# Moving the first weight tiles' narrowing, the first key loads and the first one-hots in a clustered attention with two feed-forward blocks

## The chip, the core and the metric

The kernel runs on one core of one Trainium2 chip. The metric is the device time in microseconds (us). A core has TensorE (PE in the rows; its weight loads are PEld), VectorE (DVE), ScalarE (ACT), GpSimd (POOL) and SyncE (SP), which here only issues transfers. Each engine runs its own instructions in their order and waits on semaphores for the others. "q" behind an engine's name in a row (SPq) is its sequencer, which issues transfers.

## What is computed

The reference, cut to what matters (B=2, H=8, S=768, D=64, 16 clusters; the weights arrive as float64):

```python
q_n, k_n, c_n = (x / (norm(x) + 1e-6) for x in (q, k, centroids))
q_assign = argmax(einsum('bhsd,hcd->bhsc', q_n, c_n), -1)   # k_assign likewise
mask = q_assign[:, :, :, None] == k_assign[:, :, None, :]
scores = where(mask, scale * q @ k.T, -1e9)
x = softmax(scores) @ v                                     # to [1536, 512]
x = softplus(x @ w_in) @ w_out                              # d_ff 2048
out = (silu(x @ w_gate) * (x @ w_val)) @ w_out2             # d_ff 1536
```

## The kernel before

A float32 product runs as three products of a split: x = hi + lo, and hi·hi + hi·lo + lo·hi are summed. A split is a copy to hi and a subtraction for lo.

**Attention** goes over 8 pairs of heads (`NP`), 12 tiles of 128 queries to a pair, 96 tiles in all (`N_IT`, index i). `step(i)` writes out, in this order: the scores of tile i on TensorE (`sc`, L466) and their row maximum on VectorE (L474); the exponentials of tile i-1 on ScalarE (`ex`, L482); the six transposes of tile i-2 on TensorE (`tr`, L498), split by ScalarE (`th`, L504) and VectorE (`tl`, L505); the events that a table `at` holds for i (what later pairs need); and a part of the product with the values (`pv`, L515). The program's order on each engine is that in which this code is written.

**The first pair** is prepared ahead of the loop. SyncE issues the loads of the centroids (`cn`, L272), of the first queries `qn` and keys `kn` (`load_qk(0)`, L254) and of the first weight tile `raw` (L94). VectorE and ScalarE normalize the centroids (L301 to L312; two of the steps, L305 and L306, are ScalarE's). TensorE transposes q, then the centroids (`cps`, L318), then k (L340); 12 small products with the centroids (`sims`, L377) follow, q's six and then k's six, into one PSUM tile; between these groups stand 17, 1, 6, 9, 3 and 1 transposes of a constant (`warm`, L280). VectorE splits q and k (L352, L353) and then makes the one-hots of q's and k's clusters in five instructions over both (`prep_arg`, L401 to L423). TensorE transposes the one-hots (`ohps`, L622), VectorE and ScalarE copy them to their places (L627 to L634), and the scores of tile 0 can start.

**Weights** are loaded as bits of float64 and made to float32 in two steps by the generator `w_narrow`: the first step is one ScalarE instruction (L115) and two of VectorE (L116, L119); the second is two of VectorE (L123, L126), the copy to hi (L135, VectorE) and the subtraction for lo (L136, GpSimd). The steps of all tiles stand in a queue `todo`; `pump(n)` writes out the next n. In the attention loop `pump(2)` stands behind tiles 0 and 26 (L708), so that two of the tiles of `w_in` are ready when attention ends; a second step also issues the load of a further tile.

**The feed-forward blocks** (L731, L813, L913) follow and are not touched.

Of the kernel before, what the change touches and what calls it, by code (L numbers as in the profile page):

```python
# [11 lines left out]
F32 = mybir.dt.float32  # L12
# [4 lines left out]
ALU = mybir.AluOpType  # L17
AX = mybir.AxisListType
PSUM = bass.MemoryType.PSUM

# A score of a query and a key of different clusters.  A power of two whose
# unit in the last place is far above any score, so that it swallows the score.
FAR = 2.0 ** 100

# The high words of 2^-126 and of the largest float32 as float64, read as float32.
F64_LEAST = struct.unpack("f", struct.pack("I", 0x38100000))[0]
# [3 lines left out]
def _r(t):  # L30
    """The float32 view of a float32r tile, for engines that read it as data."""
    return t.bitcast(F32)


def _h(ap, n=2):
    """[p, n*m] -> [p, n, m]"""
    return ap.rearrange("p (a n) -> p a n", a=n)
# [3 lines left out]
def kernel(  # L41
# [12 lines left out]
):  # L54
    """Every float32 product runs as float32r products: x = hi + lo exactly, both
    parts being float32r, and hi*hi + hi*lo + lo*hi is accumulated.

    Token order on chip: column b*768 + t*128 + p is token b*768 + 6*p + t.
    """
    nc = tc.nc  # L60
# [26 lines left out]

# [1 line left out]
    def w_load(w, rows, cols):  # L89
# [12 lines left out]
    def w_narrow(loaded):  # L102
        """float64 bits [p, a, f, 2] (low word, high word) -> float32 [p, a, f], in two steps

        For 2^-126 <= |x| < 2^128 the float32 exponent is the top bit and the low
        seven bits of the eleven; magnitudes below and above are brought to that
        range's ends first."""
        raw, shape, wide = loaded
        if not wide:
            yield  # L110
            yield raw
            return
        lo, hi = raw[:, :, :, 0], raw[:, :, :, 1]
        m = wp.tile(shape, I32, tag="m", name="m", bufs=2)
        nc.scalar.activation(out=m.bitcast(F32), in_=hi.bitcast(F32), func=AF.Abs)  # L115
        nc.vector.tensor_scalar(  # L116
            out=m.bitcast(F32), in0=m.bitcast(F32), scalar1=F64_LEAST, scalar2=F64_MOST, op0=ALU.max, op1=ALU.min
        )
        nc.vector.tensor_scalar(  # L119
            out=m, in0=m, scalar1=3, scalar2=0x3FFFFFF8, op0=ALU.logical_shift_left, op1=ALU.bitwise_and  # L120
        )
        yield
        nc.vector.scalar_tensor_tensor(  # L123
            out=m, in0=hi, scalar=-0x40000000, in1=m, op0=ALU.bitwise_and, op1=ALU.bitwise_or
        )
        nc.vector.scalar_tensor_tensor(  # L126
            out=m, in0=lo, scalar=29, in1=m, op0=ALU.logical_shift_right, op1=ALU.bitwise_or
        )
        yield m.bitcast(F32)
# [14 lines left out]

    # units of the two feed-forward blocks; a unit's own tiles are split three units
    # ahead, the tile of the output product with the unit
    NU = NF1 + NF2
# [12 lines left out]

    # the first tiles of the second block's values have room early on
    early = {NF1 - 14 + 3 * i: ("val", i) for i in range(3)}
# [22 lines left out]
    def split_tasks(batch):  # L185
        """two steps for each tile"""
        steps = {}

        def first(key):
            while key not in loaded_t:  # L190
                load_ahead(len(loaded_t) + 1)
            steps[key] = w_narrow(loaded_t.pop(key))
            next(steps[key])

        def second(key, tag):
            x = next(steps[key])
            load_ahead(3)
            pool, bufs = pool_of[tag]
            W[key] = w_split(x, pool, tag, bufs)

        tasks = []
        for key, _, tag in batch:
            tasks.append(functools.partial(first, key))
            tasks.append(functools.partial(second, key, tag))
            begun.add(tasks[-1])
        return tasks

    # work of the other engines that is emitted between parts of the products
    todo = collections.deque()

    def first_do(tasks):
        """before all others, but for the second step of a tile whose first was done"""
        begun_one = [todo.popleft()] if todo and todo[0] in begun else []
        todo.extendleft(reversed(begun_one + tasks))
# [10 lines left out]

    # ================= attention =================
    actx = ExitStack()
# [10 lines left out]

    # operands of the scores, one set per head in flight:
    # Q: [q_lo; -FAR*(1-onehot); 0] and [q_hi; q_hi]  # L240
    # K: [k_hi; onehot; 0] and [k_hi; k_lo]
    NB = 4
# [5 lines left out]
    def load_qk(pr, which=(0, 1)):  # L248
        b, m = divmod(pr, NPAIR)
        for n in which:  # L250
            src, dst, nm = ((q, qn_t, "qn"), (k, kn_t, "kn"))[n]
            t = pre.tile([128, NT, 2, D], F32, tag=nm, name=nm)
            for hh in range(2):
                nc.sync.dma_start(  # L254
                    out=t[:, :, hh, :],
                    in_=src[b, 2 * m + hh].rearrange("(p t) d -> p t d", t=NT),
                )
# [12 lines left out]
    cnc2 = one.tile([128, S], F32, tag="xa0", name="cnc2")  # L270
    cn, c2 = cnc2[:, 0:D], cnc2[:, D:2 * D]
    nc.sync.dma_start(out=cn, in_=centroids.rearrange("h c d -> (h c) d"))  # L272
    load_qk(0)
    load_ahead([1, 1, 3][0])

    def warm(n):
        """the tensor engine's clock rises with its use"""
        ps = ps_o.tile([128, 512], F32, tag="o", name="warm")
# [4 lines left out]

    # constants
    ohs = one.tile([4 * C, 2], F32, name="ohs")
# [12 lines left out]

    # centroids over their norms; the block diagonal of a pair of heads
    ss = one.tile([128, 4], F32, name="ss")  # L300
    nc.vector.tensor_tensor(out=c2, in0=cn, in1=cn, op=ALU.mult)  # L301
    nc.vector.tensor_reduce(out=ss[:, 0:1], in_=c2, axis=AX.X, op=ALU.add)
    nc.vector.tensor_scalar_max(ss[:, 0:1], ss[:, 0:1], 1e-37)
    # a square root to float32's accuracy: an estimate and a Newton step
    nc.scalar.activation(out=ss[:, 1:2], in_=ss[:, 0:1], func=AF.Ln)  # L305
# [16 lines left out]

# [1 line left out]
    xr_t, y_t, eq_t, oh_t, OH_t, VV_t, hl_t = {}, {}, {}, {}, {}, {}, {}  # L324
# [60 lines left out]
    def prep_sims(pr, which, spread=True):  # L385
        """spread: between the transposes of a step"""
        if which == 0:
# [7 lines left out]
    def prep_arg(pr, step):  # L395
        """the one-hot of the first of the largest"""
        full = [128, 4 * NT, C]
# [55 lines left out]

# [1 line left out]
    N_IT = NP * 2 * NT  # L455
    CT = 2                  # query tiles to a chunk of P V
    CW = 128 * CT
# [122 lines left out]

    # the first pair's; its one-hots get 32 partitions to a head, so that they are copied
    # to their places by the engines
    oh0 = two.tile([128, NT, CW], F32R, tag="tl", name="oh0").rearrange("p t n -> p (t n)")[:, 0:128 * NT]
# [16 lines left out]
    khl = two.tile([128, NT, CW], F32R, tag="th", name="khl").rearrange("p t n -> p (t n)")  # L600
    prep_split(0, 1, nc.vector, (khl[:, 0:S], khl[:, S:2 * S]))
    for which in range(2):
# [5 lines left out]
    load_ahead([1, 1, 3][2])  # L608
    # and the start of the second pair's
    mpool[0] = (ps_t, "t")  # L610
# [4 lines left out]
    mpool[0] = (ps_m, "m")  # L615
    for n in range(4):
        prep_arg(0, n)
    for half in range(2):
# [84 lines left out]
    for i in range(N_IT + 1):  # L703
        step(i)
        if i == N_IT - 12:
            rctx.close()
            pool_of["b"] = (ctx.enter_context(tc.tile_pool(name="bp", bufs=4, side="right", reuse_waits="tile")), 4)
        if i in (0, 26):  # L708
            pump(2)
    rec(NP - 1)  # L710
    rec_rows(NP - 1)
    sctx.close()

    # ================= the two feed-forward blocks =================
    psa = tc.tile_pool(name="psa", bufs=4, space=PSUM, side="right", reuse_waits="tile")
# [9 lines left out]
    def proj(xh, xl, w, banks, kks):  # L725
        """banks[c] += (x @ w)^T over the slices kks, for 512 tokens each"""
        hi, lo = w
# [10 lines left out]

    # the first products start with the pairs of heads that are done
    h0 = [bank() for _ in range(NCH)]  # L740
# [31 lines left out]

    # block 1: y^T = softplus(x w_in) w_out
    acc = mp.tile([128, KD, NTOK], F32, tag="acc", name="acc")
# [76 lines left out]

    # block 2: out = (silu(y w_gate) * (y w_val)) w_out2
    acc2 = mp.tile([128, NTOK // 128, DM], F32, tag="acc", name="acc2")
# [88 lines left out]
# Bass has no float64: such an input goes in as its bits, and is narrowed on the chip.  # L942
_INS = ['q', 'k', 'v', 'centroids', 'moe_w_in', 'moe_w_out', 'moe2_w_gate', 'moe2_w_val', 'moe2_w_out']
# [26 lines left out]
```

## Time and profile before

| | us |
|---|---|
| three runs | 860.93, 862.71, 866.04; median 862.71 |
| the profiled execution, from its first to its last instruction (the only time that is on record of it) | 861.7 |
| TensorE busy in it | 820.9 (95%) |
| VectorE, ScalarE, GpSimd busy | 683.9, 397.6, 336.0 |

Times inside the execution count from its first instruction. The attention loop's first scores stand at 18.3 us. A row of a timeline gives start, duration, engine, line, operation, output and inputs, shapes, the count of merged instructions, and in brackets how long the engine had been idle before and what ended that.

### The profile page before, as it was taken

Reading aid. Unit: us, or ns where it says so; the run is one execution under the profiler, and the core shown is the slowest. Engines: PE = TensorE matmul, PEld = TensorE weight load, DVE = VectorE, ACT = ScalarE, POOL = GpSimd, SP = SyncE. Lnnn points to the kernel's source line nnn. Section 1 sums busy time; section 2 is a strip of 40 time slices with the busy share of each in tenths; the row PEclk is TensorE's granted clock in tenths of the full one; section 3 lists DMA queues with packets and bytes.
Section 4 is the critical chain, followed back from the end, with each engine's and each line's share of the span. In section 5 each row is a group of like instructions: output and inputs, shape, how many; then the busy total and the mean of one; then the engine's idle time right before and its main releaser. Section 6 shows DMA issues by size and latency. Waiting matters only on the chain.

```text
span 861.7 us, 11737 instructions
## 1 busy us (share of the span) xinstructions
PE 820.9 (95%) x4366; PEld 697.5 (81%) x4366; DVE 683.9 (79%) x1016; ACT 397.6 (46%) x735; POOL 336.0 (39%) x229
## 2 busy tenths in 40 slices
PE   7999999999999999989898997799999999999998
PEld 6899999999898778768777786588888888888886
DVE  6888978988896778898888888849886868876464
ACT  4689889888893755433244433232212212120210
POOL 3636465555522545444244333424433312332110
PEclk9799999999999999999999999999999999999999
DMA  8975775575312132122221120202312221220003
GB/s 200 248 163 134 190 150 142 141 172 122 85 38 69 49 98 74 51 74 80 65 74 50 49 74 25 68 7 74 97 50 74 74 73 49 74 72 26 1 1 146
DMA packets 65336, 75.42 MB, mean 88 GB/s; under 512 B 28960, under 2 KB 51584, under 8 KB 65280
## 3 DMA queue, kind: packets, MB, share of 16 engines
q1 hardware_dynamic: 65280, 74.68, 32.3%
q8 instruction: 34, 0.56, 0.3%
q14 instruction: 22, 0.18, 0.1%
HBM read 48.27 MB, written 3.19 MB: 60 GB/s over the span
## 4 chain that ended last, share of the span: by engine, by line
PE 60%; DVE 25%; DMA 5%; issue 4%; ACT 4%; POOL 1%; SPq 0%; POOLq 0%; ACTq 0%; DVEq 0%
PE bank L731 28%; PE bank L913 11%; PE sps L466 5%; PE ops L515 5%; DVE m L116 5%; PE tps L498 5%; DVE acc L827 5%; DVE e L796 3%; PE bank L813 2%; DVE r L789 2%; DVE m L126 2%; DVE m L123 2%; DMA rd<-rt 2%; DMA R<-rd 2%; DVE whi L135 2%
## 5 line engine op out<-in xcount | busy, mean ns | idle before, releaser
L136 POOL TENSOR_TENSOR wlo<-m,whi 128x512 fp32r<-128x512 f32 x68 | 100.7, 1480 | 291.9 <-DVE whi L135 266.1
L116 DVE TENSOR_SCALAR m<-m 128x512 f32<-128x512 f32 x68 | 86.0, 1265 | 38.4 <-ACT m L115 38.4
L505 DVE TENSOR_TENSOR tl<-tps,th 128x384 fp32r<-128x384 f32 x192 | 98.8, 550 | 20.2 <-ACT th L504 19.6
L474 DVE TENSOR_REDUCE nm<-sps 128x1 f32<-128x768 f32 x96 | 91.3, 952 | 14.3 <-PE sps L466 11.4
L498 PE MATMUL tps<-id,p 128*128 128x128 f32 x576 | 95.3, 282 | 1.1 <-DVE tl L505 1.1
L504 ACT CAST th<-tps 128x384 fp32r<-128x384 f32 x192 | 84.6, 491 | 20.1 <-PE tps L498 17.1
L482 ACT ACTIVATE p<-sps,nm 128x768 f32<-128x768 f32 x96 | 88.1, 918 | 5.6 <-DVE nm L474 5.6
L466 PE MATMUL sps<-KT,QT 128*128 128x384 f32 x384 | 84.7, 343 | 5.6 <-ACT p L482 3.7
L731 PE MATMUL bank<-YH,whi 128*128 128x512 f32 x288 | 81.6, 391 | 2.5 <-DVE acc L827 2.5
L498 PEld LDWEIGHTS tps<-id,p 128*128 128x128 f32 x576 | 76.4, 153 | 8.4 <-DVE tl L505 5.1
L731 PE MATMUL bank<-YL,whi 128*128 128x512 f32 x288 | 81.6, 392 | 0.0
L731 PE MATMUL bank<-YH,wlo 128*128 128x512 f32 x288 | 81.6, 392 | 0.0
L769 ACT CAST gh<-e 128x1536 fp32r<-128x1536 f32 x16 | 23.7, 1481 | 122.8 <-DVE e L796 122.8
L515 PE MATMUL ops<-th,VV 128*128 128x256 f32 x288 | 79.7, 306 | 0.0
L813 PE MATMUL bank<-gh,whi 128*128 128x512 f32 x192 | 58.9, 407 | 17.3 <-DVE r L789 8.2
L115 ACT ACTIVATE m<-raw 128x512 f32<-128x512 f32 x68 | 44.5, 666 | 62.1 <-POOL wlo L136 62.0
L515 PE MATMUL ops<-tl,VV 128*128 128x256 f32 x288 | 71.9, 279 | 0.0
L770 POOL TENSOR_TENSOR gl<-e,gh 128x1536 fp32r<-128x1536 f32 x16 | 57.1, 3573 | 34.5 <-ACT gh L769 30.7
L466 PEld LDWEIGHTS sps<-KT,QT 128*128 128x128 f32 x384 | 63.4, 191 | 6.7 <-ACT p L482 4.4
L731 PEld LDWEIGHTS bank<-YH,whi 128*128 128x128 f32 x288 | 54.4, 189 | 14.3 <-issue 2.9
L731 PEld LDWEIGHTS bank<-YH,wlo 128*128 128x128 f32 x288 | 54.5, 189 | 11.4
L731 PEld LDWEIGHTS bank<-YL,whi 128*128 128x128 f32 x288 | 54.5, 189 | 11.3
(124 smaller groups left out, 1776.6 us busy)
## 6 DMA issues: line engine op xcount, KB each, us to landing
raw<-in_moe_w_out_dram SPq DMA_DIRECT2D x28, 512.0 KB, 3.3
raw<-in_moe_w_in_dram SPq DMA_DIRECT2D x16, 512.0 KB, 3.9
QT<-hi SPq DMA_DIRECT2D x32, 192.0 KB, 3.1
raw<-in_moe_w_val_dram SPq DMA_DIRECT2D x12, 512.0 KB, 4.0
raw<-in_moe_w_gate_dram SPq DMA_DIRECT2D x12, 512.0 KB, 3.5
KT<-hi SPq DMA_DIRECT2D x14, 384.0 KB, 5.8
qn<-in_q_dram SPq DMA_DIRECT2D x16, 192.0 KB, 5.7
kn<-in_k_dram SPq DMA_DIRECT2D x16, 192.0 KB, 4.2
```

The source lines that it names most:

```text
L116: nc.vector.tensor_scalar(out=m.bitcast(F32), in0=m.bitcast(F32), scalar1=F64_LEAST, scalar2=F64_MOST, op0=ALU.max, op1=ALU.min)
L136: nc.gpsimd.tensor_tensor(out=lo, in0=x, in1=_r(hi), op=ALU.subtract)
L466: nc.tensor.matmul(ps[:, c, 0:384], lhsT=Q[:, a, 128 * j:128 * j + 128], rhs=K[:, a, 384 * c:384 * c + 384], start=(a == 0), stop=(a == 1),)
L474: nc.vector.tensor_reduce(out=nm, in_=ps[:, :, 0:384], axis=AX.XY, op=ALU.max, negate=True)
L482: nc.scalar.activation(out=_h(p), in_=s_t.pop(i)[:, :, 0:384], func=AF.Exp, bias=nm_t.pop(i), accum_out=sm_t[pr][:, j:j + 1],)
L498: nc.tensor.transpose(ps[:, 128 * j:128 * j + 128], p[:, 128 * kb:128 * kb + 128], id32)
L504: nc.scalar.copy(th, pv)
L505: nc.vector.tensor_tensor(out=tl, in0=pv, in1=_r(th), op=ALU.subtract)
L515: nc.tensor.matmul(o[:, 0:CW], lhsT=VV_t[pr][:, hh, kb].rearrange("p a d -> p (a d)"), rhs=t[:, kb, :], start=(kb == 0 and lohi == 0), sto ...
L731: nc.tensor.matmul(banks[c], lhsT=wt[:, kk, :], rhs=xt[:, kk, 512 * c:512 * c + 512], start=(kk == 0 and wt is hi and xt is xh), stop=(kk ...
L813: nc.tensor.matmul(banks[NCH * d + c], lhsT=wt[:, 0, ds_], rhs=gt[:, 512 * c:512 * c + 512], start=(ff == 0 and n == 0), stop=(ff == 1 and ...
L913: nc.tensor.matmul(bk, lhsT=lhs[:, ts_], rhs=rhs[:, 0, :], start=(ff == 0 and n == 0), stop=(ff == 1 and n == 2),)
```

## The change

Three edits (the diff also empties comments, which is left out here). The loads of the first keys are issued by ScalarE, the rest by SyncE, with the centroids behind the queries. Of the first keys' split, lo is GpSimd's; and the first one-hots are made by a new function `first_arg`, called once for q and once for k, each time with the same five operations over half the columns. The narrowing steps stand one by one behind tiles 6, 9, 29 and 32, where two each stood behind tiles 0 and 26.

```diff
@@ load_qk @@
-                nc.sync.dma_start(
+                (nc.scalar if pr == 0 and n else nc.sync).dma_start(
...
+    load_qk(0)
     nc.sync.dma_start(out=cn, in_=centroids.rearrange("h c d -> (h c) d"))
-    load_qk(0)
     load_ahead([1, 1, 3][0])
...
-    prep_split(0, 1, nc.vector, (khl[:, 0:S], khl[:, S:2 * S]))
+    hl_t[0, 1] = khl[:, 0:S], khl[:, S:2 * S]
+    nc.vector.tensor_copy(khl[:, 0:S], xr_t[0, 1])
+    nc.gpsimd.tensor_tensor(out=khl[:, S:2 * S], in0=xr_t[0, 1], in1=_r(khl)[:, 0:S], op=ALU.subtract)
...
+    def first_arg(which):
+        full = [128, NT, 2, C]
...
+        nc.vector.tensor_reduce(out=mx, in_=y, axis=AX.X, op=ALU.max)
+        nc.vector.tensor_tensor(out=eq, in0=y, in1=mx.to_broadcast(full), op=ALU.is_equal)
...
+        nc.vector.tensor_reduce(out=mx, in_=eq, axis=AX.X, op=ALU.max)
+        nc.vector.tensor_tensor(out=oh, in0=eq, in1=mx.to_broadcast(full), op=ALU.is_equal)
...
-    for n in range(4):
-        prep_arg(0, n)
+    for which in range(2):
+        first_arg(which)
...
-        if i in (0, 26):
-            pump(2)
+        if i in (6, 9, 29, 32):
+            pump(1)
```

SyncE's queue at the program's start, before and after (`cnc` holds the centroids, `raw` the first weight tile; the semaphores are named in brackets). Before:

```order
L272 DMA cnc_104<-in_centroids_dram 128x64
L254 DMA qn<-in_q_dram 128x6x64 x2
L254 DMA kn<-in_k_dram 128x6x64 x2
L94 DMA raw<-in_moe_w_in_dram 128x4x256
L254 DMA qn<-in_q_dram 128x6x64 [waits DMAHW2_49,DMAHW1_49,PE_49]
```

After:

```order
L254 DMA qn<-in_q_dram 128x6x64 x2
L273 DMA cnc_104<-in_centroids_dram 128x64
L94 DMA raw<-in_moe_w_in_dram 128x4x256
L254 DMA qn<-in_q_dram 128x6x64 [waits DMAHW1_49,DMAHW0_49,PE_49]
L254 DMA qn<-in_q_dram 128x6x64
```

The centroids moved behind the queries; the first keys are gone from this queue and stand on ScalarE's, behind its table load and ahead of its first activation (L305).

VectorE between the split of the first keys and the copies of the one-hots (`mx` the maxima, `eq` the comparison, `oh` the one-hots; `PE_49` is TensorE's semaphore). Before:

```order
L352 CAST khl<-xr 128x768 [waits Activation_49]
L353 TENSOR_TENSOR khl<-xr,khl 128x768 [waits DVE_49]
L401 TENSOR_REDUCE mx<-sims 128x24 [waits PE_49]
L407 TENSOR_TENSOR eq<-sims,mx 128x384 [waits DVE_49]
L412 TENSOR_TENSOR eq<-eq,wi 128x384 [waits DVE_49,Pool_49]
L416 TENSOR_REDUCE mx_298<-eq 128x24 [waits DVE_49]
L423 TENSOR_TENSOR oh_178<-eq,mx_298 128x24x16 [waits DVE_49,Pool_49]
```

After:

```order
L602 CAST khl<-xr 128x768 [waits Activation_49]
L613 TENSOR_REDUCE mx<-sims 128x6x2 [waits PE_49]
L614 TENSOR_TENSOR eq<-sims,mx 128x6x32 [waits DVE_49]
L615 TENSOR_TENSOR eq<-eq,wi 128x6x32 [waits DVE_49,Pool_49]
L618 TENSOR_REDUCE mx<-eq 128x6x2 [waits DVE_49]
L619 TENSOR_TENSOR oh_178<-eq,mx 128x6x2x16 [waits DVE_49,Pool_49]
L613 TENSOR_REDUCE mx<-sims 128x6x2
L614 TENSOR_TENSOR eq<-sims,mx 128x6x32 [waits DVE_49]
L615 TENSOR_TENSOR eq<-eq,wi 128x6x32 [waits DVE_49]
L618 TENSOR_REDUCE mx<-eq 128x6x2 [waits DVE_49]
L619 TENSOR_TENSOR oh_178<-eq,mx 128x6x2x16 [waits DVE_49]
```

Ten instructions stand where five stood; the first of q's waits for TensorE, the first of k's for nothing.

VectorE in tiles 8 to 10 of the kernel after (`nm` the row maximum of the scores, `tl` the low part of the transposed exponentials):

```order
L474 TENSOR_REDUCE nm<-sps 128x1
L505 TENSOR_TENSOR tl<-tps,th 128x3x128 x2
L123 SCALAR_TENSOR_TENSOR m<-raw,m 128x512
L126 SCALAR_TENSOR_TENSOR m<-raw,m 128x512
L135 CAST whi<-m 128x512
L474 TENSOR_REDUCE nm<-sps 128x1
```

The second step stands between two tiles' work here; before, it stood with the first step between the row maxima of tiles 0 and 1.

## Rows read from the trace of the kernel before

**Rows 1.** The page: the span, and each engine's busy time.
```profile
span 861.7 us, 11737 instructions
PE 820.9 (95%) x4366; PEld 697.5 (81%) x4366; DVE 683.9 (79%) x1016; ACT 397.6 (46%) x735; POOL 336.0 (39%) x229
```
**Rows 2.** Stretches: length, busy of five engines, TensorE's granted clock, DMA share, GB/s.
```profile
5.00:10.00 5.00, 4.28 (x32) 3.51 (x30) 2.77 (x5) 2.20 (x6) 3.16 (x5) 1.00 0.92 223
23.60:33.84 10.24, 8.76 (x42) 8.44 (x42) 7.46 (x12) 5.00 (x12) 6.18 (x6) 0.50 1.03 293
```
**Rows 3.** Timeline of the start: SyncE's first transfers.
```profile
0.74 0.39 SPq L272 DMA_DIRECT2D cnc<-in_centroids_dram  x1
1.18 1.35 SPq L254 DMA_DIRECT2D qn<-in_q_dram  x2
2.58 1.34 SPq L254 DMA_DIRECT2D kn<-in_k_dram  x2
```
**Rows 4.** The chain that ended last, at the start: start, duration, what.
```profile
1.90 3.73 DMA qn<-in_q_dram
```
**Rows 5.** Timeline: first and last step on the centroids, and their transpose.
```profile
2.64 0.23 DVE L301 TENSOR_TENSOR cnc<-cnc 128x64 f32<-128x64 f32 x1 [0.50 <-DMA cnc<-in_centroids_dram]
4.83 0.55 DVE L312 TENSOR_SCALAR cnc<-cnc,ss 128x64 f32<-128x64 f32 x1
7.22 0.30 PE L318 MATMUL cps<-id,cnc 128*64 128x128 f32 x1
```
**Rows 6.** Timeline: similarities, first and last one-hot instruction, transposes of the one-hots.
```profile
9.07 2.76 PE L377 MATMUL sims<-C,xr 128*128 128x32 f32 x24
11.87 0.56 DVE L401 TENSOR_REDUCE mx<-sims 128x24 f32<-128x384 f32 x1 [0.79 <-PE sims L377]
14.38 0.56 DVE L423 TENSOR_TENSOR oh<-eq,mx 128x384 fp32r<-128x384 f32 x1
15.53 0.83 PE L622 MATMUL ohps<-idr,oh 128*128 128x128 f32 x6
```
**Rows 7.** Timeline of the first tiles: scores of tiles 0, 1 and 3; the narrowing's first and last on VectorE.
```profile
18.33 1.95 PE L466 MATMUL sps<-KT,QT 128*128 128x384 f32 x8 [1.84 <-DVE KT L631]
20.48 0.41 DVE L116 TENSOR_SCALAR m<-m 128x512 f32<-128x512 f32 x1
23.20 1.10 DVE L135 CAST whi<-m 128x512 fp32r<-128x512 f32 x1
26.25 1.65 PE L466 MATMUL sps<-KT,QT 128*128 128x384 f32 x4 [1.48 <-ACT p L482]
```
**Rows 8.** Timeline about tile 27, with the other narrowing in one piece.
```profile
88.37 0.86 PE L466 MATMUL sps<-KT,QT 128*128 128x384 f32 x4
88.72 0.43 DVE L116 TENSOR_SCALAR m<-m 128x512 f32<-128x512 f32 x1
89.65 0.69 DVE L123 SCALAR_TENSOR_TENSOR m<-raw,m 128x512 int32<-128x512 int32 x1
91.10 0.43 DVE L135 CAST whi<-m 128x512 fp32r<-128x512 f32 x1
91.54 0.86 PE L466 MATMUL sps<-KT,QT 128*128 128x384 f32 x4
92.91 1.01 PE L498 MATMUL tps<-id,p 128*128 128x128 f32 x6 [0.51 <-DVE tl L505]
```
**Rows 9.** Stretches from scores to scores, about tiles 6, 10, 29 and 32; columns as in Rows 2.
```profile
36.64:38.69 2.05, 2.05 (x17) 2.02 (x17) 2.05 (x5) 2.01 (x6) 1.61 (x2) 1.00 1.09 176
45.50:47.89 2.39, 2.39 (x21) 2.35 (x20) 1.95 (x4) 2.39 (x8) 0.00 (x0) 1.00 0.21 39
94.63:97.08 2.45, 2.45 (x18) 1.98 (x18) 2.45 (x6) 1.93 (x4) 1.91 (x3) 1.00 0.98 242
101.20:103.76 2.56, 2.56 (x21) 2.14 (x20) 2.56 (x5) 2.52 (x7) 0.70 (x1) 1.00 0.03 11
```
**Rows 10.** The chain: a similarity product between transposes, in two places.
```profile
28.11 0.27 PE sims L377 x2
86.17 0.14 PE sims L377 x2
```

More of the change, by code (lines that the diff above doesn't have):

```diff
@@ L600 @@
     khl = two.tile([128, NT, CW], F32R, tag="th", name="khl").rearrange("p t n -> p (t n)")
-    prep_split(0, 1, nc.vector, (khl[:, 0:S], khl[:, S:2 * S]))
+    hl_t[0, 1] = khl[:, 0:S], khl[:, S:2 * S]
+    nc.vector.tensor_copy(khl[:, 0:S], xr_t[0, 1])
+    nc.gpsimd.tensor_tensor(out=khl[:, S:2 * S], in0=xr_t[0, 1], in1=_r(khl)[:, 0:S], op=ALU.subtract)
+    mx0 = two.tile([128, NT, 2, 2, 1], F32, tag="mx", name="mx")
+    eq0 = pre.tile([128, NT, 2, 2, C], F32, tag="eq", name="eq")
+    def first_arg(which):
+        full = [128, NT, 2, C]
+        y = y_t[0][:, 0:384].rearrange("p (t w h c) -> p t w h c", w=2, h=2, c=C)[:, :, which]
+        oh = oh_t[0].rearrange("p (t w h) c -> p t w h c", w=2, h=2)[:, :, which]
+        mx, eq = mx0[:, :, which], eq0[:, :, which]
+        nc.vector.tensor_reduce(out=mx, in_=y, axis=AX.X, op=ALU.max)
+        nc.vector.tensor_tensor(out=eq, in0=y, in1=mx.to_broadcast(full), op=ALU.is_equal)
+        nc.vector.tensor_tensor(
+            out=eq, in0=eq, in1=wi.unsqueeze(1).unsqueeze(1).to_broadcast(full), op=ALU.mult
+        )
+        nc.vector.tensor_reduce(out=mx, in_=eq, axis=AX.X, op=ALU.max)
+        nc.vector.tensor_tensor(out=oh, in0=eq, in1=mx.to_broadcast(full), op=ALU.is_equal)
     for which in range(2):
```

## The prediction, written before the changed kernel was run

> **What bounds the kernel now.** I read the page first: TensorE is busy 95% of the span [rows 1], so a change pays only where TensorE waits, or where its clock is down, or where it puts off TensorE's first scores. Then the timeline of TensorE with its idle times: in the loop up to tile 36 there are few. It waits 1.84 us ahead of the first scores for the one-hots, 1.48 us ahead of tile 3 [rows 7], and 0.51 us behind the second narrowing [rows 8]. The wait ahead of tile 3 is the narrowing's work: VectorE runs it from 20.48 to 24.30 us, between the row maxima of tiles 0 and 1, so the exponentials of tile 1 come late. Last the granted clock by stretches: from 23.60 to 33.84 us it is 0.50, which is 1.2 GHz and not 2.4; TensorE is busy 8.76 of these 10.24 us, so at the full clock it would have needed 4.38 us less [rows 2]. From there on the loop is TensorE's, tile after tile in 2.05 to 2.56 us, with VectorE and ScalarE close behind: in the stretches about tiles 6, 29 and 32 VectorE has no idle time, about tile 10 it has 0.44 us [rows 9]. The feed-forward blocks don't change, and the narrowed tiles are wanted only there.
>
> **The start: the loads.** Before, the centroids are issued first, at 0.74 us, and VectorE has them at 2.64 [rows 3, 5]; they are ready at 5.38 (4.83 + 0.55), 2.74 us after they landed, and wait until 7.22 for TensorE, so this chain has 1.84 us to spare. After, they are issued behind q, and TensorE must transpose them ahead of the keys: keys that land sooner gain nothing while the centroids are missing. When do they land? The second half of q lands at 5.63 (1.90 + 3.73) [rows 4]. The issue of q moves up by 0.44 us (1.18 - 0.74), so q lands at 5.19 if the keys on the other queue don't disturb it; the 32 KB of the centroids take another 0.14 us at 223 GB/s [rows 2], 5.33 us. That is the low end. If q's and k's transfers, now issued side by side, share the DMA engines evenly, q's 393 KB (two loads of 768x64 float32) move at half the rate and take 1.76 us longer (393 KB at 223 GB/s): 7.09 us. That is the high end; the DMA share of 0.92 in that stretch says that there is little room left, so I take a value nearer to it, 6.4 us. Add 2.74 for the chain: ready at 8.07 to 9.83, taken 9.14. So TensorE's transpose moves from 7.22 by +0.9 to +2.6 us, **taken +1.9**. Behind it stand k's transposes, the warm-up transposes and the similarities, in order, and none of them gets shorter. ScalarE's evacuation of q also stands behind the two centroid steps on ScalarE (L305, L306), which now wait longer; that is inside the same 1.9.
>
> The Trainium skill (DMA: Bandwidth & Descriptors, section Issuing engines are not separate DMA queues) says that transfers issued by different engines run on the same 16 DMA engines and interleave, and that a second issuer saves only issue time. By that alone the high end would hold, and the sum below would be 0.7 us more. No row here has two issuers, so the trace neither agrees nor disagrees.
>
> **The start: the one-hots.** Five instructions take from 11.87 to 14.94 us (14.38 + 0.56), 3.07 us, each 0.56 us on 384 columns [rows 6]. An instruction on 64 columns takes 0.23 us [rows 5]; on 192 columns I put 0.36 us (0.23 + 128/320 of the 0.33 between), and with 0.04 us between two, ten take 4.0 us: **+0.9 us** (0 if half the columns cost half, +1.2 at most). It could be won back only if q's half started while TensorE still makes k's similarities. The order says no: the first instruction on q's half waits for TensorE, that on k's half for nothing more, so the one wait covers both halves and both start when the last similarity is done. The subtraction for the keys' lo leaves VectorE, but VectorE idled 0.79 us ahead of the one-hots [rows 6], so that saves nothing; on GpSimd it ends long before the transfers need it. Against these stands one piece of cover: the transposes of the one-hots started 0.59 us after the one-hots were ready (15.53 - 14.94), because the second pair's keys were late. Those move less than the one-hots now, so this is taken off. The first scores move by 1.9 + 0.9 - 0.6 = **+2.2 us** (+0.3 to +3.2).
>
> **The first tiles.** Without the narrowing, VectorE's row maximum of tile 1 follows that of tile 0 at once, and the 1.48 us that TensorE waited ahead of tile 3 go [rows 7]. What is late next there is TensorE itself. If the clock falls at the same place, these 1.48 us are filled with work at half rate and are worth half: **-0.75 us**. If it does not fall, 4.38 us come on top of the 1.48: -5.9 us. Which? Ahead of 23.60 TensorE had a wait for the first exponentials and then scores and transposes in the same order as after the change; the edit takes away only what came later. So I take the fall as staying, and the other as a rival.
>
> **Tiles 6 and 9.** Behind tile 26 the whole narrowing held VectorE from 88.72 to 91.53 us, 2.8 us, and TensorE waited 0.51 [rows 8]: 2.3 us of cover, at a tile that took 3.17 us (91.54 - 88.37), long because of similarities between the transposes. The tiles at 6 and 10 take 2.05 and 2.39 us [rows 9], so the cover is 1.1 and 0.8 us less: 1.2 and 1.5 us. The first step is 0.9 us of VectorE (88.72 to 89.65 with its gaps), the second 1.9 us (89.65 to 91.53). At tile 6 VectorE has no idle time and another one-hot instruction of 0.5 us comes at tile 7: 0.9 + 0.5 - 1.2, some 0.2 to 0.3 us of waiting, and VectorE is still behind by about 0.5 us when the second step comes: 1.9 + 0.5 - 1.5 = 0.9. Together **+1.2 us** (0.2, if idle time such as the 0.44 us about tile 10 takes most of it, to the whole 2.8). ScalarE's one instruction of a first step lies beside VectorE's backlog.
>
> **Tiles 29 and 32.** The same way: tiles of 2.45 and 2.56 us [rows 9] leave 1.6 and 1.7 us of cover. The first step is hidden; of the second, with 0.4 us of one-hot backlog, 0.6 us show. The 0.51 us at tile 26 go. **+0.1 us** (-0.5 to +1.5). The weight loads that the second steps issue only move later on SyncE's queue, and nothing waits for them before the feed-forward blocks.
>
> **The sum** is 2.2 - 0.75 + 1.2 + 0.1 = +2.75 us on the profiled span of 861.7: 864.5 us. The median of the runs lies 1.0 us above that span, so I forecast **865.5 us** against 862.71.
>
> **The rivals.**
> (a) **The clock holds** through the first tiles. For it: TensorE's work is denser there without the wait ahead of tile 3. Against it: what came ahead of 23.60 stays. 2.2 - 5.9 + 1.3 = -2.4: 860.3 us.
> (b) **The costs are small**: the centroids land at the low end, or the steps at 6, 9, 29 and 32 vanish in VectorE's idle time as 2.3 of 2.8 us did at tile 26. Sum near +0.9: 863.6 us. Against it: rows 9 show VectorE without idle time in three of the four places.
> (c) **Slower: TensorE's clock is down in the start.** Place: TensorE now stands idle some 1.9 us longer between q's transposes and the centroids'. If the clock is at 1.2 GHz behind that, k's transposes and the similarities run at half rate; a similarity pair takes 0.27 us there against 0.14 [rows 10]. The similarities alone take 2.76 us [rows 6], with the transposes around them some 4.6, of which I charge 3.5: 869.0 us. It decides from the point where the granted clock between 9 and 16 us reads well below 1.00.
> (d) That the change does not do what it says is in the forecast in one part: the one-hots are written apart but can't start apart.
>
> **How the numbers follow.** Forecast 0.40, (a) 0.27, (b) 0.19, (c) 0.14. Around each case I allow about 2 us, the spread of the unknown terms. A measurement of this kernel can tell about 0.5%, 4.3 us, from no change. Faster than 858.4: the tail of (a), 0.05, and 0.04 for what I don't see: 0.09. Slower than 867.0: most of (c), 0.12, and a fifth of the forecast case, 0.08, and a little: 0.22. Within: 0.69. The range that leaves out 2 in 10 runs from 859.0 (most of (a)) to 869.0 (half of (c)).
>
> **What would show it.** In the trace after: the transpose of the centroids near 9.1 us, not 7.2, with TensorE idle before it on VectorE's account; ten one-hot instructions of about 0.36 us that all start after the last similarity; first scores near 20.5 us; no 1.5 us wait ahead of tile 3; a stretch at clock 0.50 of about 10 us starting some 5 us after the first scores; waits of TensorE for `tl` about tiles 8 to 11 of 0.3 and 0.9 us and about tile 34. The prediction is wrong if the centroids land before 5.5 us, if q's one-hots run beside k's similarities, or if the granted clock stays at 1.00 through the first tiles.

## The result, and the profile after

| | before | after |
|---|---|---|
| median of 11 runs each, us | 863.04 | 870.74 |
| range of them | 860.93 to 866.93 | 866.67 to 874.99 |
| span of the profiled execution (its own time for after: 868.77) | 861.7 | 866.7 |
| ratio of the times, with its 95% interval | | 1.0084 (1.0061 to 1.0108) |

The changed kernel is slower by 7.3 us (5.3 to 9.3; ratio by 863). I had forecast +2.75 us, with a change of under 0.5% as likeliest (0.69); 870.7 lies above the range's end of 869.0. A second set of runs, below, gives 6.4 us. In both kernels single runs lie 6 to 8 us apart. TensorE's clock goes with that: of the eleven runs of after, the fastest has a mean granted clock of 0.991 and the slowest 0.972, and in the traces the few stretches with a fallen clock stand in other places in each profile, two profiles of one kernel included. So a price below is a ratio of times over some 12 runs; a trace tells the mechanism.

The page of after, span and busy times: TensorE's work is the same as in [rows 1], the span 5.0 us longer.

```profile
span 866.7 us, 11733 instructions
PE 821.1 (95%) x4366; PEld 697.1 (80%) x4366; DVE 685.9 (79%) x1020; ACT 398.6 (46%) x735; POOL 336.4 (39%) x230
```

VectorE's row maximum of tile 29 and of tile 37, first before and then after, by the timeline. Up to tile 29 the changed kernel is 0.2 us ahead, eight tiles later 4.65 us behind: this profile's loss arises around the steps behind tiles 29 and 32, and what the start cost it is made up by the first tiles before that.

```profile
95.96 0.94 DVE L474 TENSOR_REDUCE nm<-sps 128x1 f32<-128x768 f32 x1
115.28 0.96 DVE L474 TENSOR_REDUCE nm<-sps 128x1 f32<-128x768 f32 x1
```
```profile
95.75 0.95 DVE L474 TENSOR_REDUCE nm<-sps 128x1 f32<-128x768 f32 x1
119.93 0.96 DVE L474 TENSOR_REDUCE nm<-sps 128x1 f32<-128x768 f32 x1 [0.39 <-PE sps L466]
```

**Tiles 29 and 32**, timeline of after: VectorE's narrowing, GpSimd's work, TensorE's transposes that waited.

```profile
97.95 1.15 DVE L116 TENSOR_SCALAR m<-m 128x512 f32<-128x512 f32 x1
99.13 1.12 DVE L119 TENSOR_SCALAR m<-m 128x512 int32<-128x512 int32 x1
...
106.48 1.75 DVE L123 SCALAR_TENSOR_TENSOR m<-raw,m 128x512 int32<-128x512 int32 x1
108.26 0.69 DVE L126 SCALAR_TENSOR_TENSOR m<-raw,m 128x512 int32<-128x512 int32 x1
```
```profile
97.80 2.17 POOL L449 TENSOR_TENSOR VV<-vn,VV 128x384 fp32r<-128x384 f32 x2
100.05 1.87 POOL L548 TENSOR_TENSOR xu<-xu,xa 64x768 f32<-64x768 f32 x1
105.83 1.84 POOL L575 TENSOR_TENSOR xu<-xu,R 128x768 f32<-128x768 f32 x1 [3.92 <-DMA R<-rd]
```
```profile
101.64 1.01 PE L498 MATMUL tps<-id,p 128*128 128x128 f32 x6 [1.82 <-DVE tl L505]
...
110.80 1.01 PE L498 MATMUL tps<-id,p 128*128 128x128 f32 x6 [1.86 <-DVE tl L505]
```

In [rows 8] L116 took 0.43 us and L123 0.69, with GpSimd idle. Here L116, L119 and L123 take 1.15, 1.12 and 1.75 us, each beside a GpSimd instruction; L126, which starts after GpSimd's is over, takes its 0.69. TensorE waits 1.82 and 1.86 us.

**The start and the first tiles**: centroids' first step and transpose, first and last one-hot instruction, first scores (timeline of after; [rows 5 to 7] answer).

```profile
6.89 0.23 DVE L301 TENSOR_TENSOR cnc<-cnc 128x64 f32<-128x64 f32 x1 [4.75 <-DMA cnc<-in_centroids_dram]
9.49 0.39 PE L318 MATMUL cps<-id,cnc 128*64 128x128 f32 x1 [2.11 <-DVE C L314]
15.34 0.36 DVE L613 TENSOR_REDUCE mx<-sims 128x12 f32<-128x192 f32 x1 [2.93 <-PE sims L377]
18.89 0.36 DVE L619 TENSOR_TENSOR oh<-eq,mx 128x192 fp32r<-128x192 f32 x1
21.02 1.16 PE L466 MATMUL sps<-KT,QT 128*128 128x384 f32 x5 [0.83 <-DVE KT L650]
```

Stretches of after, columns as in [rows 2]:

```profile
9.30:12.71 3.41, 3.22 (x16) 2.98 (x16) 2.12 (x5) 1.37 (x4) 0.21 (x1) 0.50 0.38 86
23.60:33.84 10.24, 9.21 (x73) 8.49 (x74) 7.97 (x13) 7.49 (x18) 6.46 (x7) 1.00 1.03 266
111.70:115.10 3.40, 3.40 (x17) 3.30 (x15) 1.37 (x4) 2.64 (x6) 1.82 (x1) 0.50 0.25 64
```

The clock is down from 9.30 to 12.71 us, behind the 2.11 us for which TensorE stood waiting for the centroids, and stays up where it had been down before: 73 matmul records between 23.60 and 33.84 us, not 42. It falls once more at 111.7, behind the wait of 1.86 us.

### The profile page after: what moved, and what is told of

It is laid out like the page before. It is cut to its first block, busy times and chain, and to the rows that moved or that the text cites. A ratio compares the mean times of both kernels' runs of the same rounds, so it can differ in the third digit from the quotient of the medians.

```text
span 866.7 us, 11733 instructions
## 1 busy us (share of the span) xinstructions
PE 821.1 (95%) x4366; PEld 697.1 (80%) x4366; DVE 685.9 (79%) x1020; ACT 398.6 (46%) x735; POOL 336.4 (39%) x230
## 4 chain that ended last, share of the span: by engine, by line
PE 61%; DVE 27%; issue 4%; ACT 3%; DMA 3%; POOL 1%; SPq 0%; DVEq 0%; POOLq 0%; ACTq 0%
PE bank L750 27%; PE bank L932 11%; PE ops L515 6%; PE sps L466 5%; PE tps L498 5%; DVE m L116 5%; DVE acc L846 4%; PE bank L832 3%; DVE e L815 3%; DVE m L126 2%; DVE r L808 2%; DVE m L123 2%; DVE nm L474 2%; DVE tl L505 2%; PE sims L377 2%
## 5 line engine op out<-in xcount | busy, mean ns | idle before, releaser
L116 DVE TENSOR_SCALAR m<-m 128x512 f32<-128x512 f32 x68 | 86.9, 1278 | 38.5 <-ACT m L115 38.4
L474 DVE TENSOR_REDUCE nm<-sps 128x1 f32<-128x768 f32 x96 | 91.4, 953 | 15.5 <-PE sps L466 12.8
```

Of the source, the lines that this page charges most:

```text
L116: nc.vector.tensor_scalar(out=m.bitcast(F32), in0=m.bitcast(F32), scalar1=F64_LEAST, scalar2=F64_MOST, op0=ALU.max, op1=ALU.min)
L474: nc.vector.tensor_reduce(out=nm, in_=ps[:, :, 0:384], axis=AX.XY, op=ALU.max, negate=True)
```

## The experiments

The prices are ratio minus one, by the median of before beside it (864 us), with the 95% interval in brackets. All diffs are against the kernel before. **Theory A**: three prices (a late start, some tenths at tiles 6 and 9, and steps that run beside GpSimd's work at 29 and 32). The rivals B to G stand in the expectations.

### The narrowing's steps alone, then each tile's alone

All four steps:

```diff
-        if i in (0, 26):
-            pump(2)
+        if i in (6, 9, 29, 32):
+            pump(1)
```

> The kernel before with the narrowing's steps alone moved (one behind each of tiles 6, 9, 29, 32); loads and one-hots as before. Theory A (three places, three prices): the start costs 2.6 us, the way from tile 0 to 12 gives back 4.85 - 2.9 = 2 us, tiles 29 and 32 cost 4 us net of what tile 26 had. Without the start this kernel is then about 2 us slower than before, 865, and its own first scores stand at 18.3 us; the clock holds at 1.00 through the first tiles because the narrowing's wait is gone there. Rival B: the clock held in the changed kernel because its start was later, not because the narrowing had left tile 0. Then the clock falls here as before, 4.4 us of the gain are missing, and the time is about 869. Rival C: all of the loss sits in the start; then this kernel is not slower than 863.

Measured: 865.71 us, +1.1 (-0.1 to +2.4). That speaks against rival B's 869; between theory A's +2 and nothing (rival C) it does not decide. In this profile the clock fell at 20.4 us, which rival B had foretold and theory A had not, so the gain in the first tiles that theory A counted on was missing, while the steps at 29 and 32 still cost what they do below.

The first tile's alone:

```diff
-        if i in (0, 26):
+        if i in (26,):
             pump(2)
+        if i in (6, 9):
+            pump(1)
```

> The kernel before with only the first narrowing moved: one step behind tile 6, one behind 9, two behind 26 as before. Theory A: the clock holds in the first tiles (worth 4.85 us with the wait ahead of tile 3), tiles 6 to 12 cost 2.9: 861, 2 us faster than before. Rival B (the clock falls all the same): only the wait's 0.75 us are gained: about 865.

Measured: 865.51 us, +1.5 (+0.3 to +2.6), near rival B's 865 and not faster. The profile shows the fall of rival B, earlier and longer: it comes right behind a wait of 2.05 us ahead of the first scores. The stretch of it:

```profile
18.90:35.90 17.00, 16.07 (x68) 15.31 (x69) 8.97 (x13) 7.54 (x16) 7.07 (x8) 0.50 1.06 252
```

The second tile's alone:

```diff
-        if i in (0, 26):
+        if i in (0,):
             pump(2)
+        if i in (29, 32):
+            pump(1)
```

> The kernel before with only the second narrowing moved: two steps behind tile 0 as before, one behind 29, one behind 32. Theory A: the first instructions of each step run beside GpSimd's and take 1.1 to 1.8 us in place of 0.43 and 0.69, TensorE waits about 1.8 us behind each, the clock falls once more for 3.4 us (1.7 us of work lost): about 867, 4 us slower than before. My prediction's own term was 0.1 us: 863.1. If the clock's fall is not there, about 865.5.

Measured: 866.77 us, +2.4 (+1.3 to +3.6). The rows of after come back: L116 1.13, L119 1.12 and L123 1.24 us, waits of 1.81 and 1.07 us, and a fall of 3.4 us at 99.8 us. My term of 0.1 us lies outside the interval.

```profile
99.47 1.36 PE L498 MATMUL tps<-id,p 128*128 128x128 f32 x6 [1.81 <-DVE tl L505]
109.01 1.01 PE L498 MATMUL tps<-id,p 128*128 128x128 f32 x6 [1.07 <-DVE tl L505]
```

### Is it GpSimd, or has VectorE no room there?

```diff
-        if i in (0, 26):
+        if i in (0,):
             pump(2)
+        if i in (27, 30):
+            pump(1)
```

> As the kernel that moves the second narrowing alone, but with its single steps behind tiles 27 and 30, where the trace of the changed kernel has GpSimd idle (92.4 to 95.9 and 101.9 to 105.8 us). The tiles are as short there, about 2.3 us, and VectorE has as little idle time. Theory A (the loss at 29 and 32 is that of running beside GpSimd): each instruction takes its short time, 0.43 or 0.69 us, TensorE waits under 1 us in all, and the time is within 1.5 us of before. Rival D (VectorE has no room there, whatever GpSimd does): the same loss as behind 29 and 32, about 4 us.

Measured: 870.34 us, +5.1 (+3.5 to +6.7). Theory A's 1.5 is out, and rival D's 4 lies in the interval; but the test was not what it was meant to be, since the second step met GpSimd after all: tile 30 comes earlier in this kernel. The rows still tell the two apart, as one step ran free and the other not:

```profile
92.40 0.43 DVE L116 TENSOR_SCALAR m<-m 128x512 f32<-128x512 f32 x1 [0.37 <-ACT m L115]
...
99.74 2.22 DVE L123 SCALAR_TENSOR_TENSOR m<-raw,m 128x512 int32<-128x512 int32 x1
```
```profile
99.56 1.84 POOL L548 TENSOR_TENSOR xu<-xu,xa 64x768 f32<-64x768 f32 x1
```
```profile
94.68 1.01 PE L498 MATMUL tps<-id,p 128*128 128x128 f32 x6 [0.40 <-DVE tl L505]
104.53 1.54 PE L498 MATMUL tps<-id,p 128*128 128x128 f32 x6 [3.12 <-DVE tl L505]
```

The free first step costs a wait of 0.40 us, the held one at tile 29 of after 1.82; L116 and L119 together took 1.41 us longer there (1.15 + 1.12 - 0.86), which is the difference. Why this kernel loses more than the one with the steps behind 29 and 32 is not settled; its profile shows the longest wait, 3.12 us, and a fall of 6.8 us behind it.

The direct test adds GpSimd work beside the narrowing behind tile 26, and changes nothing else:

```diff
+        if i == 26:
+            beside = pre.tile([4 * C, S], F32R, tag="OH", name="beside")
+            for _ in range(2):
+                nc.gpsimd.tensor_tensor(
+                    out=_r(beside), in0=_r(QT[0])[0:4 * C, 0, :], in1=nm_t[i][0:4 * C].to_broadcast([4 * C, S]), op=ALU.mult
+                )
         if i in (0, 26):
             pump(2)
```

> The kernel before, with two GpSimd multiplications of 64x768 into a buffer that nobody reads, started by the row maximum of tile 26, so that they lie beside the narrowing behind tile 26, where GpSimd stood idle for 5.94 us. Nothing waits for them but GpSimd's own later work. Theory A: VectorE's five instructions there take 1 to 1.8 us each where they overlap, the narrowing grows from 2.8 to some 5 us, and TensorE's wait of 0.51 us to about 2.5: 865, 2 us slower. Rival D: the narrowing takes 2.8 us as before and the time does not move, 863.

Measured: 865.96 us, +1.6 (-0.1 to +3.3). Timeline of this kernel: GpSimd's two, VectorE's first two, TensorE's wait, which was 0.51 us in [rows 8].

```profile
88.91 3.00 POOL L711 TENSOR_TENSOR beside<-QT,nm 64x768 f32<-64x768 f32 x2 [1.45 <-DVE nm L474]
```
```profile
90.50 1.70 DVE L116 TENSOR_SCALAR m<-m 128x512 f32<-128x512 f32 x1
92.23 0.43 DVE L119 TENSOR_SCALAR m<-m 128x512 int32<-128x512 int32 x1
```
```profile
95.96 1.01 PE L498 MATMUL tps<-id,p 128*128 128x128 f32 x6 [1.79 <-DVE tl L505]
```

Only L116 overlaps, and it ends 0.29 us after GpSimd (92.20 against 91.91). It takes 1.27 us more, and TensorE's wait grows by 1.28. The mechanism is shown in the rows; the time's interval alone would just allow zero.

### The start: all of it, its two halves, and the two halves of the loads

```diff
-                nc.sync.dma_start(
+                (nc.scalar if pr == 0 and n else nc.sync).dma_start(
...
+    load_qk(0)
     nc.sync.dma_start(out=cn, in_=centroids.rearrange("h c d -> (h c) d"))
-    load_qk(0)
...
-    for n in range(4):
-        prep_arg(0, n)
+    for which in range(2):
+        first_arg(which)
```

> The kernel before with the loads and the one-hots changed, and the narrowing where it was (two steps behind tiles 0 and 26). Theory A: first scores 2.6 us later, 20.9; clock down in the start from about 9.3 to 12.7 us as in the changed kernel, and down again in the first tiles as before, since the narrowing is there: about 865.5. Rival B: the later start keeps the clock up in the first tiles: 861. Rival C: the whole loss is the start's: 870.

Measured: 867.96 us, +3.5 (+2.0 to +4.8). The price lies between theory A's and rival C's and is nearer to A's. But its profile has the clock down far longer than A had it, from 7.9 to 21.6 us and again from 31.8 to 38.6, and first scores at 24.16, not 20.9.

The loads alone (the first two pieces of this diff):

> The kernel before with the loads alone changed: first keys on ScalarE's queue, the centroids behind the queries. Theory A: the centroids land at 6.9 us, their transpose starts at about 9.5 in place of 7.2, the clock is down from about 9.3 to 12.7 us, first scores 1.7 us later (2.56 less the 0.84 of the one-hots): 864.7. Rival: the keys land sooner and make up for it, 863.

Measured: 867.16 us, +3.0 (+1.6 to +4.5); transpose of the centroids at 9.44 behind 1.77 us of waiting, clock 0.50 from 9.2 to 12.6, first scores at 20.09. That is theory A's mechanism; the price is above A's without excluding it, and the rival's is out.

The one-hots alone (the last piece, with the keys' lo on GpSimd):

> The kernel before with the one-hots alone changed (two sets of five instructions, the keys' lo on GpSimd). Theory A: ten instructions take 3.9 us in place of 3.07, 0.59 us of it covered by the late keys of the second pair: first scores 0.3 to 0.8 us later, 863.5. Rival: the queries' half starts while the keys' similarities still run, and the first scores move up by about 0.5 us: 862.5.

Measured: 864.20 us, -0.4 (-2.0 to +1.0), which does not tell the two apart. The cover was as I had worked it out: TensorE's transposes of the one-hots start at 15.70, 0.17 us later than in [rows 6]. The first scores then wait for the keys' transfer, in this profile until 17.86, no later than before:

```profile
15.70 0.68 PE L641 MATMUL ohps<-idr,oh 128*128 128x128 f32 x6 [0.65 <-DVE oh L619]
17.86 3.04 PE L466 MATMUL sps<-KT,QT 128*128 128x384 f32 x8 [1.35 <-DMA KT<-khl]
```

Keys on ScalarE's queue, centroids still first:

```diff
-                nc.sync.dma_start(
+                (nc.scalar if pr == 0 and n else nc.sync).dma_start(
```

> The kernel before with the first keys issued by ScalarE, and the centroids first on SyncE's queue as before. The loads alone cost 3.0 us. Theory F (it is the order: the centroids behind the queries put off their transpose and leave TensorE idle ahead of it): here the centroids land at 2.6 us as before, their transpose is not waited for, the keys land no later, and nothing is lost: 863.5 to 864.5. Rival G (it is the second issuer: queries and keys moving side by side both land late): q lands at 6.3 us in place of 5.63, the first scores move by about 0.7 us and the loss is 1 to 3 us.

Measured: 864.77 us, +1.0 (-0.7 to +2.5). Theory F's "lands no later" was wrong: the queries are late by the second issuer. The first keys are issued from 0.77 us, not 2.58, and TensorE's transposes of q end their wait at 7.38, in the trace of before at 5.76. Between F's loss of nothing and G's of 1 to 3 us the time does not decide.

```profile
2.69 0.22 DVE L301 TENSOR_TENSOR cnc<-cnc 128x64 f32<-128x64 f32 x1 [0.54 <-DMA cnc<-in_centroids_dram]
```
```profile
7.38 0.85 PE L340 MATMUL mps<-id,qn 128*128 128x128 f32 x6 [2.12 <-DMA qn<-in_q_dram]
```

Centroids behind, all on SyncE's queue:

```diff
-    nc.sync.dma_start(out=cn, in_=centroids.rearrange("h c d -> (h c) d"))
     load_qk(0)
+    nc.sync.dma_start(out=cn, in_=centroids.rearrange("h c d -> (h c) d"))
```

> The kernel before with the centroids issued behind queries and keys, all on SyncE's queue. Theory F: the centroids land with or behind the keys, at 7 us or later, their transpose starts at about 9.7 us, the first scores are about 2 us late, and the time is 3 us or more above before: 867. Rival G: without the second issuer the loss is small: 864.5.

Measured: 867.40 us, +2.9 (+1.4 to +4.3). This order alone (here the centroids stand behind the keys too) brings back the loads' whole price and the wait for the centroids:

```profile
6.97 0.23 DVE L301 TENSOR_TENSOR cnc<-cnc 128x64 f32<-128x64 f32 x1 [4.82 <-DMA cnc<-in_centroids_dram]
```
```profile
9.57 0.27 PE L318 MATMUL cps<-id,cnc 128*64 128x128 f32 x1 [2.86 <-DVE C L314]
```

The order is the main price; the second issuer's is at most 2.5 us, perhaps nothing.

### The changed kernel again, and with one part undone

> The changed kernel once more, for a second profile and times beside the same runs of before as the next three. In the ten profiles so far TensorE's clock fell for 3.4 to 17 us within the first 36 us, in a different place in each kernel, and between 2 and 4 times in the feed-forward blocks, so one profile's clock there may be a draw and not the kernel's own. Theory A: the work itself repeats (centroids' transpose about 9.5 us, ten one-hots, GpSimd beside the narrowing at tiles 29 and 32), while the clock in the first tiles is down in this profile for some microseconds, unlike in the first one. Rival E: the clock holds again from 12.7 us to tile 30; then holding belongs to the change. Time about 870.5, 6 to 7 us above before.

Measured: 869.71 us, +6.4 (+4.2 to +8.6; 6 runs). Both theories were half right. The work repeats. The clock is low over most of the start (the similarities take 5.17 us, not 2.76 as in [rows 6], and its record first reads 1.00 at 21.1), so the first scores come 2.6 us later than in the first profile; but in the first tiles it holds again. It was low before the wait for the centroids: the transposes of q ahead of it take 1.51 us, against 0.85 in the first profile.

```profile
6.85 1.51 PE L340 MATMUL mps<-id,qn 128*128 128x128 f32 x6 [1.60 <-DMA qn<-in_q_dram]
...
12.41 5.17 PE L377 MATMUL sims<-C,xr 128*128 128x32 f32 x24
...
23.64 1.68 PE L466 MATMUL sps<-KT,QT 128*128 128x384 f32 x8 [0.69 <-DVE KT L650]
```
```profile
23.60:33.84 10.24, 8.71 (x67) 8.14 (x68) 7.88 (x12) 7.58 (x17) 5.18 (x6) 1.00 1.00 259
```

The loads undone (one-hots and steps as changed):

> The changed kernel with its loads undone: centroids first, all on SyncE's queue; one-hots and single steps as changed. The loads alone cost 2.7 to 3.0 us, the one-hots alone nothing (-0.3), the steps alone 1.5. If the costs add, this kernel is 1.2 us above before, 865.5, and 5 us below the changed kernel. If the parts work on each other (the three alone add up to 4.3 to 4.5 us, the change cost 7.3), it lies in between, at about 867.5: then the missing part sits between the one-hots and the steps.

Measured: 867.10 us, +2.8 (+1.3 to +4.3), 3.6 us below the changed kernel beside it, in between the two values named.

The second tile's steps undone (start, and tiles 6 and 9, as changed; two steps behind tile 26):

> The changed kernel with two steps behind tile 26 in place of one each behind 29 and 32; start and tiles 6 and 9 as changed. Theory A: without GpSimd beside these steps the two waits of about 1.8 us at 29 and 32 go and the 1.1 us at 26 come back: 2.4 us (as when these steps alone were moved) to 4 us faster than the changed kernel, 867. My prediction's term says 0.1 us: 870.5.

Measured: 867.06 us, +3.5 (+1.9 to +4.9), 2.9 us below the changed kernel beside it, as theory A had it. L116 to L135 take their short times there and TensorE waits 0.51 us, as in [rows 8].

### One step a pair, in long tiles

```diff
-        if i in (0, 26):
-            pump(2)
+        if i in (14, 26, 38, 50):
+            pump(1)
```

> The kernel before with the four steps one by one behind tiles 14, 26, 38 and 50, which are the first of the two long tiles of a pair (3.2 us, similarities between the transposes), where VectorE has idle time of 0.24 to 0.56 us between its instructions and GpSimd is idle behind its merge. Theory A: the steps take their short times (0.43, 0.69 us), each is covered, TensorE waits under 0.3 us at each; the wait of 1.48 us ahead of tile 3 and the 1.1 us at tile 26 go: 862, some 2 us faster than before. Rival D: a step costs about 0.5 us wherever it stands; no faster than 864.

Measured: 864.86 us, +0.8 (-0.5 to +2.1): not faster. Three of the four steps ran free (two are shown); the third met GpSimd, and its L116 took 2.10 us at 120.28, behind which TensorE waited 0.28 us. The first tiles ran at the full clock, and by the row maximum of tile 35 the profile is 2.5 us ahead of before. Then TensorE waits for ScalarE's copy of a later pair's queries, 0.88 us in the trace of before and 1.97 here, and the clock falls for 3.4 us behind it; at tile 37 the lead is gone.

```profile
56.52 0.43 DVE L116 TENSOR_SCALAR m<-m 128x512 f32<-128x512 f32 x1
...
86.73 0.68 DVE L123 SCALAR_TENSOR_TENSOR m<-raw,m 128x512 int32<-128x512 int32 x1
```
```profile
18.50:40.00 21.50, 18.89 (x143) 17.18 (x141) 17.50 (x29) 16.22 (x37) 9.84 (x11) 1.00 1.03 241
110.70:114.10 3.40, 3.40 (x16) 3.27 (x16) 2.90 (x5) 3.13 (x9) 2.75 (x4) 0.50 0.51 111
```
```profile
109.27 0.55 PE L340 MATMUL mps<-id,qn 128*128 128x128 f32 x3 [1.97 <-ACT xr L343]
```

No version that I ran is shown to beat the kernel before.

## Why the prediction was wrong, step by step

**Tiles 29 and 32: the step that failed.** Forecast +0.1 us (-0.5 to +1.5); measured +2.4 (+1.3 to +3.6) alone, and 2.9 in what undoing it gives back. The sum of durations took L116 at 0.43 and L123 at 0.69 us from [rows 8], where GpSimd was idle. At 29 and 32 it is not, and those three instructions took 4.02 us where I had charged 1.55. The waits of 1.82 and 1.86 us are what I forecast (0.6 in all) plus that difference of 2.5, to within 0.6 us. At tile 29 it was readable beforehand: [rows 9] show GpSimd busy 1.91 of 2.45 us, and the same L135 took 1.10 us in [rows 7] and 0.43 in [rows 8]. I took the one row for the duration and did not ask what the other stood beside. At tile 32 it was not readable: there GpSimd is busy 0.70 of 2.56 us, and the instruction that the second step met (L575) waits for a transfer and started at 107.50 us in before, at 105.83 in after. The Trainium skill (SBUF — State Buffer, section Who interferes with whom) names a cause: VectorE and GpSimd have one pair of ports in common, which one instruction holds for its whole length while the other waits. It says this of VectorE instructions in a two-port mode, which copies, casts and tensor_scalar can enter, and of those with two inputs in SBUF if the GpSimd one reads SBUF; the reduction is exempt. The rows agree: in the test at tile 26, L116 ends 0.29 us after GpSimd's second multiplication, and in after the row maximum at 100.17 us, beside L548, takes 0.94 us as ever.

**The start.** Forecast +2.2 us, measured +3.5 (+2.0 to +4.8), which does not exclude 2.2. The loads' mechanism held: VectorE had the centroids at 6.89 us (forecast 6.4, between 5.33 and 7.09), the transpose came at 9.49 (forecast 9.1). The experiments put the price on their order. The Trainium skill's rule on issuing engines, which I had set beside it (DMA: Bandwidth & Descriptors, section Issuing engines are not separate DMA queues), is borne out: TensorE's first transposes of q start at 6.34 to 7.38 us in the six profiles with two issuers and at 5.22 to 5.92 in the ten with one, and the earlier issue of the keys won no time. The one-hots took ten times 0.36 us, 3.91 in all (forecast 4.0). Their cover of 0.59 us was there when they were changed alone. In the first profile of the changed kernel it was not: the second pair's keys were not waited for, TensorE waited for the one-hots, and its first scores came 0.9 us later than with the loads alone (first row after, second row the loads alone):

```profile
19.39 0.68 PE L641 MATMUL ohps<-idr,oh 128*128 128x128 f32 x6 [1.43 <-DVE oh L619]
```
```profile
20.09 2.04 PE L466 MATMUL sps<-KT,QT 128*128 128x384 f32 x8 [0.82 <-DVE KT L631]
```

What was mis-sized is the clock, and that was rival (c), to which I gave 0.14. In all six profiles with the centroids behind (the two of the changed kernel, the start alone, the loads alone, the centroids behind, the second tile undone) TensorE works at the lower level for 3.4 us or more between 7 and 21.6 us; of the ten others, before included, four show that before their first scores. In the second profile of the changed kernel the price of (c) came in full: 3.5 us on top of 20.5 gives 24.0, and the first scores stood at 23.64. Its cause did not: there the clock was low already before the wait for the centroids.

**The first tiles.** Forecast -0.75 us with the fall staying; rival (a), 0.27, had the clock hold. Its mechanism came true in both profiles of the changed kernel, and with it one of the prediction's own signs of being wrong. The wait ahead of tile 3 went as forecast; one ahead of tile 2, which the prediction leaves out, stayed (1.35 us at 21.64 before, 1.48 at 24.20 after). Of nine profiles with the narrowing at tile 0, eight have a fall that begins between 22.6 and 31.8 us; of the seven without it, five have none from 21 to 100 us. The other two had fallen at 18.9 and 20.4, behind waits of over 2 us for the first scores. So the fall goes with the narrowing at tile 0, but not with it alone; that the wait brings it is not shown by itself. In the changed kernel the start costs about what the first tiles gain: at tile 29 the first profile is 0.2 us ahead of before, the second 0.85 behind. (a) erred in the rest of its sum.

**Tiles 6 and 9.** Forecast +1.2 us of waiting. The second profile shows 0.71 and 0.43 us, 1.1 together; the first 0.42 and one of 1.53. That one is the same contention, on a one-hot instruction that I had taken at 0.5 us (timeline of after):

```profile
39.64 1.80 POOL L353 TENSOR_TENSOR lo<-xr,hi 128x768 fp32r<-128x768 f32 x1
39.70 2.16 DVE L423 TENSOR_TENSOR oh<-eq,mx 128x384 fp32r<-128x384 f32 x1
```

It is not the steps' alone: with tiles 29 and 32 moved and the narrowing at tile 0 the same wait is 1.15 us. Together with the first tiles the forecast was +0.45, the measurement +1.5 (+0.3 to +2.6), which does not exclude the forecast.

**The sum.** The three parts measured alone give 3.5 + 1.5 + 2.4 = 7.4 us, the change 7.3 and 6.4. Of the 4.6 us that I missed by this sum, 2.3 are tiles 29 and 32, 1.3 the start, 1.0 the first tiles with 6 and 9; only for tiles 29 and 32 does the forecast lie outside the measured interval. One thing stays open: the steps alone cost 1.1 us (up to 2.4), less than the 3.9 of their halves. If I let the four parts (loads, one-hots, first tile, second tile) add up, and fit all ten ratios weighted by their intervals, they come out at 3.4, 0.1, 0.6 and 1.9 us, each by about 0.5; the kernel with the steps alone lies two of its standard errors below that. Whether that is scatter or a true interplay through the clock, these runs don't settle.

## What to carry to other kernels

A duration belongs to the place where it was read: before work is moved on VectorE, look at what GpSimd does at the new place, and take the long duration if two rows of one line differ. A small transfer that a long chain hangs on goes first in its queue, ahead of large ones. A wait of TensorE of 1 to 2 us costs more than itself where a fall of the clock follows it, and behind which of several waits it falls changed from profile to profile, so such a term needs a range of its own.

## What the runs showed of the hardware that I had not expected

- L116, L119 and L123 on VectorE, starting while a GpSimd instruction runs, were held until that one had ended: 1.12 to 1.70 us for L116 and L119 in after and in the test at tile 26 (0.43 alone), up to 2.22 for L123 (0.69 alone). The row maximum (L474) was not held.
- The falls of the clock are not tied to a place in the program: two profiles of the changed kernel have it up at 1.00 from 12.7 to 111.7 us and from 21.1 to 103.0, and in the feed-forward blocks, which are the same in all, the sixteen profiles have two to five falls.
- A second issuer starts the keys 1.8 us earlier (0.77 for 2.58) and shows no gain in time (+1.0 us, -0.7 to +2.5), while the queries beside them come 1.6 us later (7.38 for 5.76).
